# Gated mix of attention and SwiGLU: both parts of a weight made by GpSimd instead of ScalarE and GpSimd

## The chip, the cores and the metric

The kernel runs on one core of a Trainium2 chip. The metric is the device time of one execution in microseconds; several executions are timed and the median is given. One more execution is recorded by the profiler, and all rows shown come from such recordings. The engines of a core are TensorE (PE, with PEld for its weight loads), VectorE (DVE), ScalarE (ACT), GpSimd (POOL) and SyncE (SP), each with an instruction queue of its own that is worked off in order.

## What is computed

The input x has 2048 rows of 640 numbers. One branch is causal attention with 32 heads of 20 numbers in four segments of 512 rows, each with a memory of the segments before it; the other is a SwiGLU feed-forward layer of width 1728. A gate per row mixes the two. All data is f32.

```python
x = A_x
g = _sigmoid((x * gate_w).sum(-1, keepdims=True))
a = _A_ref(x, A_wq, A_wk, A_wv, A_wo, A_beta)   # per segment: softmax attention and memory read, mixed; then @ wo
b = _B_ref(x, B_w1, B_w3, B_w2)                 # (silu(x @ w1) * (x @ w3)) @ w2
return g * a + (1 - g) * b
```

## The kernel before

**Two parts of every operand.** Projections run on PE in the type fp32r. For precision every f32 operand is split: the high part is the value rounded to fp32r, the low part is the value minus the high part. A product takes three matmuls (high by high, high by low, low by high), so each weight tile of 128 by 640 becomes a tile `W` of two parts. The helper `split` (line 115) makes them: line 116 rounds on ScalarE, line 117 subtracts on GpSimd (on VectorE for the first seven weights). The same helper splits `ht`, the product of the feed-forward layer.

**The weights' way.** There are 133 weight tiles in a fixed list of use. `w_load` (line 163) starts the DMA of a raw tile `wr` into one of two raw buffers; `w_split` (line 177) makes `W` from it in one of six slots; `w_step` (line 184) is called at every step of the projections and starts both ahead of use. A slot is free when PE has read the weight six places earlier, a raw buffer when the subtraction on GpSimd has read it. For weights from number 7 on, `w_step` also notes one of ScalarE's latest instructions (`last["exp"]`, an exponential of attention, or `last["act"]`), and `behind` (line 105) pins the cast behind it in ScalarE's queue.

**The stages.** The head projects q, v and k of the first two segments (columns "q", "v", "k"). Then attention runs over 32 groups of four heads, and the projections of both branches are woven between its steps: `g` and `u` (line 262) for the feed-forward layer's two inner products, `f` (line 543) for its outer one, `op` (line 793) for attention's. For each group PE makes scores `s` (line 590), whose row maxima VectorE takes (line 597, tile `junk`), and transposed scores `t` (line 623), whose exponentials ScalarE writes to `P` (line 629) and GpSimd masks (line 633); then `o` (line 643) multiplies `P` and v. The memory read is `nd` (line 340), and `normalize` (lines 717 to 725) scales `o`, with a transpose `gt` and a broadcast `rr` in PSUM. The heads' queries and keys `qk` are loaded by DMAs from GpSimd's queue (line 567), the row maxima `mr` by DMAs from ScalarE's (line 611). After attention a tail ends the last group.

**Order.** PE's order is the program's own. For the other engines a planner at build time sets the order in which their instructions stand in their queues, from its own estimate of when each can run. The eight PSUM banks are handed out in turn (`bank_tile`), so a matmul into a bank waits until the engine that reads its last content is done.

Of the kernel before, what the change touches and what calls it, by code (L numbers as in the profile page):

```python
# [8 lines left out]
F32 = mybir.dt.float32  # L9
# [19 lines left out]
NP, AGE = 3, 4  # L29
# [9 lines left out]
def gated_mix(ctx: ExitStack, tc: tile.TileContext, xT, wqk, wv, w13, w2, w2h, wo, beta, out):  # L39
    nc = tc.nc  # L40
# [61 lines left out]
    here = tc.keep_in_program_order  # L102
    last = {}

    def behind(ins):

        def pin(i):
            if ins is not None:
                tc.add_manual_dep(i.ins, ins.ins.name,
                                  mybir.DependencyInfo(mybir.DependencyClass.NoSync, mybir.DependencyReason.DATA),  # L110
                                  reason="behind")
            return i
        return pin

    def split(dst, src, lo=None, pin=lambda ins: ins):
        pin(nc.scalar.copy(dst[:, 0], src))  # L116
        (lo or nc.gpsimd.tensor_sub)(dst[:, 1], src, dst[:, 0].bitcast(F32))  # L117
# [44 lines left out]
    early, raws, clock = [], [], dict(step=0, oldest=0, next=0)  # L162

    def w_load():
        k = clock["next"]
        src, n, queue = items[k]
        if k in EARLY:
            if k % 2 == 0:
                early[:] = [sp.tile([P, 2, 1280], F32, tag="P32", name=f"wr{k}", bufs=NP)]
            raw = early[0][:, k % 2]  # L170
        else:
            raw = sp.tile([P, D + 2], F32, tag="wraw", name=f"wr{k}", bufs=NRAW)
        queue.dma_start(raw[:, :n], src)
        raws.append([k, raw, n, clock["step"], None])
        clock["next"] += 1

    def w_split():
        k, raw, n, _, after = raws.pop(0)
        w = sp.tile([P, 2, D + 2], FR, tag="W", name=f"W{k}", bufs=NW)
        tiles[k] = w  # L180
        split(w[:, :, :n], raw[:, :n], lo=nc.vector.tensor_sub if k < 7 else None, pin=behind(after))

    def w_step():


        clock["step"] += 1
        for r in raws:
            if clock["step"] - r[3] == (AGE // 2 if "exp" in last else 2 * AGE) and r[0] >= 7:
                r[4] = last.get("exp", last["act"])
        if raws and raws[0][0] in EARLY:  # L190
            if clock["step"] >= 6 + 2 * raws[0][0]:
                w_split()
        elif raws and raws[0][0] < clock["oldest"] + NW and \
                clock["step"] - raws[0][3] >= (AGE if "exp" in last or raws[0][0] < 7 else 2 * AGE + 1):
            w_split()
        if sum(r[0] not in EARLY for r in raws) < NRAW and clock["next"] < min(len(items), clock["oldest"] + NW + NRAW):
            w_load()

    def w_get(i, oldest=None):

        while i not in tiles:
            if not raws or raws[-1][0] < i and len(raws) < NRAW:
                w_load()
            else:
                w_split()
        clock["oldest"] = i if oldest is None else oldest
        return tiles[i]
# [6 lines left out]
    def load_first(c, n):  # L214

        for kb in range(KB):
            r = xraw[c][:, kb]
            nc.sync.dma_start(r, xT[c, :, kb, :])
            split(Xs[c][:, :, kb, :], r, lo=nc.vector.tensor_sub)
            if kb < n:  # L220
                w_load()
                w_split()
# [231 lines left out]
    def job_read(c):  # L454
        return 5.6, memory_read(c)
# [440 lines left out]
    r = job_read(2)  # L896
    up = [job_up(B, 0), job_up(B, 1)]
    seg += q[:2] + [braid(chain(q[2:]), r, 2, 7, False)]
    r = 0.6 * r[0], r[1]
# [17 lines left out]
    for n, (_, g) in enumerate(head):  # L917
        for _ in g:
            stores()
            w_step()  # L920
        if n == 0:
            constants()
        elif n == 4:
            selection()
        elif n == 9:
            gates()
# [9 lines left out]
    def step(run):  # L936
        d = next(run[1], None)
        if d is not None:
            for k in held:
                held[k] += d  # L940
            if not isinstance(d, float):
                stores()
                w_step()
        return d
# [32 lines left out]
    for _, g in tail:  # L977
        for d in g:
            if not isinstance(d, float):
                w_step()  # L980
                tick()
# [51 lines left out]
```

## Time and profile before

| | us |
|---|---|
| runs timed | 1112.77, 1113.28, 1115.76 |
| median | 1113.28 |
| profiled execution, its own time | 1111.06 |
| its span, first to last instruction | 1109.3 |
| busy: PE / PEld / DVE / ACT / POOL | 1094.8 / 853.0 / 588.4 / 461.3 / 493.8 |
| casts of weights on ScalarE (line 116), 133 | 95.7 |
| subtractions for weights on GpSimd (line 117), 126 | 197.7 |

The busy times are sums over one engine's instructions; engines run side by side. An idle time belongs to the engine in whose row it stands, and what ended it is named behind an arrow. A group's row has the line of the kernel, engine, operation, the tile written and those read (buffer numbers left out), shapes, the count, busy us, the mean ns of one, and the idle us before them with what ended it. A row of the timeline has start and duration in us, then the same, and in brackets the idle time before it.

### The profile page before, as it was taken

To read this page: it belongs to the slowest core of one execution; us is meant where nothing else is said; L and a number is where in the kernel's file an instruction comes from. 1 tells how busy PE (TensorE), PEld (TensorE's weight loads), DVE (VectorE), ACT (ScalarE), POOL (GpSimd) and SP (SyncE) were. 2 spreads that over 40 slices of the span, in tenths; PEclk is the share of its full clock that TensorE was granted. 3 is DMA by queue.
4 is the path that set the end of the run, shared out by engine and by line. 5 is a ranking of instruction groups with operands and counts; after the bars stand their busy time and mean duration, and the time that the engine had idled before them with its cause. 6 is when DMAs were issued, how large, how long until landed. Compare 5 with 4: busy or idle time off the path is not lost.

```text
span 1109.3 us, 17962 instructions
## 1 busy us (share of the span) xinstructions
PE 1094.8 (99%) x6285; PEld 853.0 (77%) x6285; DVE 588.4 (53%) x1708; ACT 461.3 (42%) x952; POOL 493.8 (45%) x603
## 2 busy tenths in 40 slices
PE   9999999999999999999999999999999999999997
PEld 6988877777777777787977777777777777777786
DVE  5032564355555554366153677874557665551645
ACT  6265344444244233265254653435543443344130
POOL 5053445355355253354163436544744455354132
PEclk9999999999999999999999999999999999999999
DMA  8265943335165233436276866454744434332123
GB/s 321 94 235 196 278 119 93 82 84 132 47 157 128 60 84 114 123 101 190 94 250 222 290 206 183 112 160 130 182 120 111 123 82 122 84 113 76 51 60 114
DMA packets 87545, 153.20 MB, mean 138 GB/s; under 512 B 11584, under 2 KB 25184, under 8 KB 87456
## 3 DMA queue, kind: packets, MB, share of 16 engines
q1 hardware_dynamic: 63040, 106.30, 30.3%
q0 software_dynamic: 20384, 38.68, 15.6%
q10 hardware_dynamic: 4032, 7.08, 1.8%
q8 instruction: 50, 0.82, 0.3%
q14 instruction: 39, 0.32, 0.1%
HBM read 96.56 MB, written 54.54 MB: 136 GB/s over the span
## 4 chain that ended last, share of the span: by engine, by line
PE 88%; DVE 4%; issue 2%; DMA 2%; ACT 2%; POOL 1%; ACTq 0%; SPq 0%; DVEq 0%; POOLq 0%
PE g L262 16%; PE f L543 16%; PE u L262 15%; PE v L373 6%; PE k L262 6%; PE q L262 6%; PE o L643 5%; PE op L793 5%; PE s L590 4%; PE t L623 3%; PE nd L340 1%; PE pm L437 1%; DVE junk L597 1%; DMA qk<-mr 1%; PE pkt L422 1%
## 5 line engine op out<-in xcount | busy, mean ns | idle before, releaser
L117 POOL TENSOR_TENSOR W<-wr,W 128x640 fp32r<-128x640 f32 (+1 forms) x126 | 197.7, 1575 | 279.3 <-ACT W L116 217.7
L597 DVE CUSTOM_DVE_ANT_0 junk<-s,mask 128x256 bf16<-128x256 f32 (+3 forms) x512 | 250.2, 489 | 106.7 <-PE s L590 73.4
L629 ACT ACTIVATE P<-t 128x512 f32<-128x512 f32 (+1 forms) x384 | 172.4, 538 | 147.9 <-PE t L623 126.3
L262 PE MATMUL g<-X,W 128*128 128x512 f32 x840 | 208.7, 398 | 1.8 <-ACT P L629 1.8
L262 PE MATMUL u<-X,W 128*128 128x512 f32 x780 | 196.8, 399 | 0.0
L543 PE MATMUL f<-ht,W 128*128 128x512 f32 x820 | 196.3, 396 | 0.0
L262 PEld LDWEIGHTS g<-X,W 128*128 128x128 f32 x840 | 155.9, 188 | 38.6 <-ACT P L629 2.0
L633 POOL TENSOR_SCALAR_AFFINE_SELECT P<-P 128x256 f32<-128x256 f32 x192 | 93.3, 496 | 201.7 <-ACT P L629 201.0
L543 PEld LDWEIGHTS f<-ht,W 128*128 128x128 f32 x820 | 152.7, 188 | 36.4
L262 PEld LDWEIGHTS u<-X,W 128*128 128x128 f32 x780 | 144.0, 188 | 34.5 <-ACT P L629 0.3
L116 ACT CAST W<-wr 128x640 fp32r<-128x640 f32 (+1 forms) x133 | 95.7, 729 | 128.7 <-DVE acc L551 26.2
L117 POOL TENSOR_TENSOR ht<-ft,ht 128x512 fp32r<-128x512 f32 x52 | 67.8, 1304 | 81.1 <-ACT ht L116 81.0
L567 POOL DMA_DIRECT2D qk<-qkd x128 | 82.8, 648 | 2.2 <-PE t L623 1.7
L590 PE MATMUL s<-qk 60*128 60x256 f32 (+3 forms) x512 | 78.0, 346 | 1.2 <-DVE fu L503 1.0
L262 PE MATMUL k<-X,W 128*128 128x512 f32 x300 | 77.1, 403 | 0.7 <-ACT P L629 0.7
L643 PE MATMUL o<-P,vg 128*32 128x512 f32 (+3 forms) x1024 | 75.5, 435 | 0.2
L262 PE MATMUL q<-X,W 128*128 128x512 f32 x300 | 74.1, 401 | 1.0 <-DVE X L117 0.5
L503 DVE SCALAR_TENSOR_TENSOR fu<-ft,g 128x512 f32<-128x512 f32 x52 | 35.6, 686 | 73.6 <-ACT ft L502 73.2
L373 PE MATMUL v<-W,X 128*128 128x320 f32 (+1 forms) x480 | 71.6, 311 | 0.4 <-ACT P L629 0.4
L373 PEld LDWEIGHTS v<-W,X 128*128 128x128 f32 x480 | 71.0, 189 | 0.8 <-ACT P L629 0.6
L551 DVE TENSOR_TENSOR acc<-f,acc 128x512 f32<-128x512 f32 x65 | 44.6, 689 | 44.8 <-PE f L543 44.6
L262 PEld LDWEIGHTS q<-X,W 128*128 128x128 f32 x300 | 55.8, 189 | 16.3 <-DVE X L117 1.1
(117 smaller groups left out, 1122.5 us busy)
## 6 DMA issues: line engine op xcount, KB each, us to landing
qk<-qkd POOLq DMA_DIRECT2D x128, 240.0 KB, 4.2
wr<-in_w_dram SPq DMA_DIRECT2D x80, 320.0 KB
qkd<-qs SPq DMA_DIRECT2D x20, 512.0 KB
qkd<-ks SPq DMA_DIRECT2D x20, 512.0 KB
od<-oq SPq DMA_DIRECT2D x32, 256.0 KB
wr<-in_wo_dram SPq DMA_DIRECT2D x20, 320.0 KB
vg<-vd SPq DMA_DIRECT2D x16, 336.0 KB
xr<-in_xT_dram SPq DMA_DIRECT2D x20, 256.0 KB
```

Source lines behind the costliest of these rows:

```text
L116: pin(nc.scalar.copy(dst[:, 0], src))
L117: (lo or nc.gpsimd.tensor_sub)(dst[:, 1], src, dst[:, 0].bitcast(F32))
L262: nc.tensor.matmul(ps, w[:, a, kb * P:(kb + 1) * P], x[:, b, kb, :], start=n == 0, stop=n == 14)
L373: nc.tensor.matmul(ps[:, :n1 - n0], x[:, a, kb, lb * P:(lb + 1) * P], wvt[kb][:, b, n0:n1], start=n == 0, stop=n == 14)
L543: nc.tensor.matmul(ps, w, h, start=n == 0, stop=n == len(ms) - 1)
L567: here(nc.gpsimd.dma_start(t[64 * i:64 * i + RH], qkd[c][RH * (h + i):RH * (h + i + 1)]))
L590: nc.tensor.matmul(ps[i][:, o:o + w], q[:, qb * P:(qb + 1) * P], key[:, :w], start=n == 0, stop=n == len(todo) - 1, skip_group_check=True)
L597: nc.vector.tensor_tensor_reduce(out=junk[:, :w], in0=ps[i][:, o:o + w], in1=mask[:, L - w:], scale=1.0, scalar=-3.0e38, op0=ALU.add, op1= ...
L629: last["exp"] = nc.scalar.activation(pairs[2 * m + k]["P"][:, i, o:o + n], ps[i][:, b:b + n], AF.Exp, scale=SCALE)
L633: nc.gpsimd.affine_select(d, d, pattern=[[0, 2], [0, n], [1, P]], base=0, channel_multiplier=-1, compare_op=ALU.is_ge, fill=0.0)
L643: nc.tensor.matmul(ps[32 * i:32 * i + 32, kb * P:], heads[2 * p + i]["v"][:, kb], pairs[p + i // 2]["P"][:, i % 2, o:o + n], start=kb == 0 ...
L793: nc.tensor.matmul(ps, ws[kb][:, b, fb * P:(fb + 1) * P], oT[a][:, kb], start=n == 0, stop=n == 14)
```

## The change

For weights from number 7 on, the rounded part is made by a copy on GpSimd, directly followed in the program by the subtraction that GpSimd made before. ScalarE keeps the casts of the first seven weights, of x and of `ht`. The pinning of casts falls away with them. 126 instructions move from ScalarE to GpSimd; the planner then sets the queues' orders anew, while PE's order stays as it is.

```diff
-    def behind(ins):
-
-        def pin(i):
-            if ins is not None:
-                tc.add_manual_dep(i.ins, ins.ins.name,
-                                  mybir.DependencyInfo(mybir.DependencyClass.NoSync, mybir.DependencyReason.DATA),
-                                  reason="behind")
-            return i
-        return pin
-
     def split(dst, src, lo=None, pin=lambda ins: ins):
         pin(nc.scalar.copy(dst[:, 0], src))
         (lo or nc.gpsimd.tensor_sub)(dst[:, 1], src, dst[:, 0].bitcast(F32))
...
     def w_split():
-        k, raw, n, _, after = raws.pop(0)
+        k, raw, n, _ = raws.pop(0)
         w = sp.tile([P, 2, D + 2], FR, tag="W", name=f"W{k}", bufs=NW)
         tiles[k] = w
-        split(w[:, :, :n], raw[:, :n], lo=nc.vector.tensor_sub if k < 7 else None, pin=behind(after))
+        if k < 7:
+            split(w[:, :, :n], raw[:, :n], lo=nc.vector.tensor_sub)
+        else:
+            nc.gpsimd.tensor_copy(w[:, 0, :n], raw[:, :n])
+            nc.gpsimd.tensor_sub(w[:, 1, :n], raw[:, :n], w[:, 0, :n].bitcast(F32))
 
     def w_step():
 
 
         clock["step"] += 1
-        for r in raws:
-            if clock["step"] - r[3] == (AGE // 2 if "exp" in last else 2 * AGE) and r[0] >= 7:
-                r[4] = last.get("exp", last["act"])
```

More of the change, by code (lines that the diff above doesn't have):

```diff
@@ L173, in w_load @@
         queue.dma_start(raw[:, :n], src)
-        raws.append([k, raw, n, clock["step"], None])
+        raws.append([k, raw, n, clock["step"]])
         clock["next"] += 1
     def w_split():
-        k, raw, n, _, after = raws.pop(0)
+        k, raw, n, _ = raws.pop(0)
         w = sp.tile([P, 2, D + 2], FR, tag="W", name=f"W{k}", bufs=NW)
         tiles[k] = w
-        split(w[:, :, :n], raw[:, :n], lo=nc.vector.tensor_sub if k < 7 else None, pin=behind(after))
+        if k < 7:
[3 more added lines that the diff above has]
+            nc.gpsimd.tensor_sub(w[:, 1, :n], raw[:, :n], w[:, 0, :n].bitcast(F32))
     def w_step():
         clock["step"] += 1
-        for r in raws:
-            if clock["step"] - r[3] == (AGE // 2 if "exp" in last else 2 * AGE) and r[0] >= 7:
-                r[4] = last.get("exp", last["act"])
         if raws and raws[0][0] in EARLY:
```

## The prediction

> **What bounds the kernel now.** I read the page's first part, then busy time by stretches, then the list of TensorE's (PE's) waits, and only then the two groups that the change touches.
>
> ```profile
> span 1109.3 us, 17962 instructions
> PE 1094.8 (99%) x6285; PEld 853.0 (77%) x6285; DVE 588.4 (53%) x1708; ACT 461.3 (42%) x952; POOL 493.8 (45%) x603
> ...
> 10.00:1100.00 1090.00, 1083.27 (x6252) 847.10 (x6252) 577.52 (x1692) 455.43 (x944) 485.77 (x585) 1.00 0.48 137
> ...
> PE g L262 <- ACT P L629: 1.8, 1, 1.8
> PE nd L340 <- ACT P L629: 1.1, 1, 1.1
> ...
> PE k L262 <- ACT P L629: 0.7, 1, 0.7
> PE t L623 <- DMA qk<-mr: 0.6, 1, 0.6
> ...
> PE v L373 <- ACT P L629: 0.4, 1, 0.4
> ```
>
> PE is busy for 1094.8 of 1109.3 us; between 10 and 1100 us (the third line; its second number is PE's busy time) it is idle for 1090.00 - 1083.27 = 6.7 us, at a granted clock of 1.00. So no relief of another engine can give more than about 6.7 us, 0.6%, and a loss has no such cap. Each row of waits reads: who waited, for whom, us in total, times, longest. Four of them, 1.8 + 1.1 + 0.7 + 0.4 = 4.0 us, are waits for ScalarE (ACT) to take the attention's exponentials (line 629) out of PSUM. No row of the list names a weight tile W: PE never waits for the thing that the change makes in another way. What the change can give is what ScalarE's casts do to its own queue.
>
> **The change, part by part.** The columns here are: engine, operation, tile and shape, count, busy us, mean ns of one, idle us before them and what ended that.
>
> ```profile
> L117 POOL TENSOR_TENSOR W<-wr,W 128x640 fp32r<-128x640 f32 x121 | 189.4, 1571 | 266.4 <-ACT W L116 209.1 <-issue 49.6 <-PE s L590 6.3
> ...
> L78 POOL CAST qk<-one 128x512 fp32r<-128x512 f32 x4 | 2.3, 602 | 0.0
> ...
> L449 POOL COPY Ms<-mt 128x147 f32<-128x147 f32 x4 | 1.2, 304 | 0.1
> ...
> L116 ACT CAST W<-wr 128x640 fp32r<-128x640 f32 x123 | 88.6, 728 | 127.4 <-DVE acc L551 26.2 <-PE u L262 24.8 <-DMA wr<-in_w_dram 19.2
> ```
>
> ScalarE loses 126 of 133 casts (the first seven weights stay): 126 x 0.73 = 92 us, and with them most of the 127 us in which it stood before a cast whose slot or raw weight was not there. GpSimd (POOL) gains 126 copies. Their price is not shown at this width. The cast of 512 columns takes 602 ns and the copy of 147 takes 304, that is 0.82 ns a column, so 640 columns take 0.71 us. The bounds: 0.60 (the 512 columns' own time) and 1.57 (the subtraction of the same tile, which reads two inputs); I take 0.71, because the cast is the same operation. GpSimd goes from 494 to 494 + 126 x 0.71 = 583 us, 53% of the span: no bound by its share. A weight's two parts take 2.28 us in one queue, where the subtraction used to follow 0.73 us of ScalarE; the 209 us that GpSimd stood waiting for ScalarE cover the difference.
>
> Now the places where PE stands still because of a cast.
>
> ```profile
> 929.43 0.73 ACT L116 CAST W<-wr 128x640 fp32r<-128x640 f32 x1
> ...
> 929.68 0.50 PE L623 MATMUL t<-qk 62*128 62x512 f32 x2
> ...
> 931.59 0.72 ACT L116 CAST W<-wr 128x640 fp32r<-128x640 f32 x1 [1.43 <-DMA wr<-in_w_dram]
> ...
> 932.22 2.18 ACT L629 ACTIVATE P<-t 128x512 f32<-128x512 f32 x6
> ...
> 932.86 1.89 PE L262 MATMUL g<-X,W 128*128 128x512 f32 x7 [1.80 <-ACT P L629]
> ```
>
> The scores t are there at about 930.2. ScalarE works in order, stands until 931.59 for a raw weight that is still on its way, casts it, and reads t only at 932.22; PE gets the bank at 932.86. Without the cast the exponentials start at 930.2, the bank is free before PE asks: 1.80 us gained.
>
> ```profile
> 749.84 0.72 ACT L116 CAST W<-wr 128x640 fp32r<-128x640 f32 x1 [0.41 <-DMA wr<-in_w_dram]
> ...
> 750.48 2.18 ACT L629 ACTIVATE P<-t 128x512 f32<-128x512 f32 x6
> ...
> 751.12 0.99 PE L340 MATMUL nd<-Ms,pq 128*128 128x84 f32 x6 [1.06 <-ACT P L629]
> ...
> 560.81 1.39 ACT L116 CAST W<-wr 128x640 fp32r<-128x640 f32 x2
> ...
> 562.05 2.23 ACT L629 ACTIVATE P<-t 128x512 f32<-128x512 f32 x6
> ...
> 562.75 1.43 PE L262 MATMUL k<-X,W 128*128 128x512 f32 x5 [0.71 <-ACT P L629]
> ```
>
> The same twice: 0.41 + 0.72 us of waiting and casting stand ahead of exponentials that PE then waits 1.06 us for; two casts of 1.39 us stand ahead of a wait of 0.71. Gained: 1.06 and 0.71.
>
> ```profile
> 500.77 0.69 DVE L525 TENSOR_TENSOR acc<-acc,sh 128x512 f32<-128x512 f32 x1 [1.69 <-DMA sh<-ed]
> ...
> 511.16 1.57 PE L623 MATMUL t<-qk 62*128 62x512 f32 x6
> ...
> 515.04 0.73 ACT L116 CAST W<-wr 128x640 fp32r<-128x640 f32 x1 [0.55 <-DMA wr<-in_wqk_dram]
> ...
> 516.91 1.89 PE L373 MATMUL v<-W,X 128*128 128x320 f32 x11 [0.42 <-ACT P L629]
> ...
> 701.53 1.28 DVE L723 TENSOR_TENSOR on<-on,gt 128x512 f32<-128x512 f32 x2
> ...
> 702.29 0.63 PE L623 MATMUL t<-qk 62*128 62x512 f32 x6
> ...
> 702.72 0.68 DVE L509 SCALAR_TENSOR_TENSOR ft<-fu,u 128x512 f32<-128x512 f32 x1
> ...
> 702.95 2.36 PE L643 MATMUL o<-P,vg 128*32 128x512 f32 x32
> 703.32 0.68 DVE L597 CUSTOM_DVE_ANT_0 junk<-s,mask 128x512 bf16<-128x512 f32 x1
> ```
>
> Outside PE the order is planned at build, and the plan moves a few VectorE (DVE) instructions too; two of these moves touch PE. First, at 511.16 six t matmuls take 1.57 us that take 0.63 at 702.29: 0.94 us behind a VectorE that is busy without a break since 500.77, where it stood 1.69 us for a transfer (sh). In the changed order two subtractions for X and an addition stand ahead of the multiplication that waits for sh, which fills that gap. With the 0.42 us at 516.91 that is 1.36; the bounds are 0.2 (only what the cast at 515.04 delays) and 1.36; I take 1.3, as the moved work, two or three times about 0.68 us, covers it. Second, a loss: at 701.53 two additions (line 723) free PE's transpose banks by 702.81, and o starts at 702.95. In the changed order the second stands behind the activation's product (L509) and a row maximum (L597): from 702.81 it ends some 0.68 + 0.68 + 0.08 = 1.4 us later, and o waits for that bank. Some of it falls into short waits that PE has anyway just behind; I take 1.0, between 0 and 1.5.
>
> GpSimd's queue is in order as well: a copy that waits for a slot holds what stands behind it. Masks and ht's low parts move by 1 to 3 us by the durations above, and nobody on PE waits for those. The loads of queries and keys are the item with a date.
>
> ```profile
> 936.87 1.29 POOL L567 DMA_DIRECT2D qk<-qkd  x2
> ...
> 952.31 0.50 PE L590 MATMUL s<-qk 60*128 60x512 f32 x2
> ...
> qk<-qkd POOLq DMA_DIRECT2D x128, 240.0 KB, 4.2
> ```
>
> With 4.2 us from issue to landing, this pair must be issued by 948.1 for the s at 952.31. It is issued at 936.87; in the changed order it stands behind both parts of two weights and most of two more, and comes, by my sum, at 947.5 and 948.1: the 11 us of slack are just used up. It costs 0 to 0.5 us; I take 0.
>
> The sum: 1.80 + 1.06 + 0.71 + 1.3 - 1.0 = 3.9 us. The profiled execution took 1111.06 us, 1.8 more than its span, which becomes 1107.2. The median of the runs shown, 1113.28, is 2.2 above it; on that level the forecast is **1109.4 us**, 0.35% faster.
>
> **A rule that speaks against it.**
>
> ```profile
> 506.77 0.68 DVE L525 TENSOR_TENSOR acc<-acc,sh 128x512 f32<-128x512 f32 x1
> ...
> 507.63 3.58 POOL L117 TENSOR_TENSOR W<-wr,W 128x642 fp32r<-128x642 f32 x2 [6.96 <-ACT W L116]
> ...
> 508.57 1.20 DVE L525 TENSOR_TENSOR acc<-acc,sh 128x512 f32<-128x512 f32 x1
> ```
>
> A VectorE product of two SBUF tiles takes 0.68 us alone and 1.20 under a GpSimd subtraction. The Trainium skill, GPSIMD Engine Reference, sections "Engine selection" and "Key points", gives ordinary elementwise work to VectorE and says that GpSimd shares its SBUF interfaces with it, so that VectorE instructions with two SBUF inputs contend; the rows agree. By that rule each such instruction that meets one of the 126 copies is late by up to 0.5 us, and one in the full stretch at 702 would make it 1109.9. By the rows of the sum it stays at 1109.4: the row maxima, which read PSUM and SBUF, are most of VectorE's time, and no copy is seen beside VectorE in this trace.
>
> **The rivals.** *The relief is given back* (0.31): PE's waits for ScalarE go, but VectorE's stretch at 500 stays, 1.80 + 1.06 + 0.71 + 0.2 = 3.8, and the moved addition at 702 costs its full 1.5 and the late load 0.5: 1.8 us gained, 1111.5. For it: two moves outside the casts decide. Against it: VectorE's gap of 1.69 us is plain.
>
> *GpSimd's queue becomes the gate* (0.17, slower): wherever three weight slots come free together, after each of the eight down projections inside attention, two weights' copies and subtractions can go ahead of a pair load. By the sum above such a load is in time at 0.71 us a copy and late by about the excess beyond it. Eight places with 0.9 us each are 7.2 us against 3.9 gained: 1113.28 + 3.3, and with the moved addition at its full 1.5, 1117. It decides from a copy of about 1.6 us, the 1.57 of the two-input subtraction; the 602 ns row of the same operation speaks against it.
>
> *The change does not do what it says*: the built order shows all 126 copies on GpSimd and none of these casts on ScalarE. I give it nothing.
>
> **How the numbers follow.** A measurement of this kernel can tell 0.3%, 3.3 us, from no change. Forecast and what lies beyond it 0.52, given back 0.31, gate 0.17; so faster 0.52, same 0.31, slower 0.17. Low end: all gains without the loss, and the 0.6 us wait for mr too, 5.5 us, and a spread of 1.3 us as the runs show it: 1106.5. High end: the gate in half of its places, with the runs' spread: 1115. The range holds both the forecast and the first rival.
>
> **What would show it.** Right: ACT about 370 us busy with seven W casts, POOL about 583 with 126 copies of 0.71 us; PE's idle time from 10 to 1100 us near 3 us; no PE wait for P above 0.5 us; the t matmuls near 511 at 0.63; o near 702 late behind line 723. Wrong: copies over 1.5 us, PE waiting for qk or W, or the waits for P still there with another holder of ScalarE.

## The result and the profile after

The changed kernel takes 1109.87 us (median of 7 runs, 1108.01 to 1111.02) where the kernel before, beside it, takes 1114.33 (7 runs, 1112.77 to 1115.76): the ratio is 0.9972, 95% interval 0.9959 to 0.9986. A second measurement gave 1109.13 against 1112.63, ratio 0.9968 (0.9955 to 0.998). The forecast was 1109.4.

The page and the stretch from 10 to 1100 us of the changed kernel (columns as in the prediction; lines stand nine lower than before, so 629 is now 620):

```profile
span 1107.7 us, 17867 instructions
PE 1094.4 (99%) x6285; PEld 852.9 (77%) x6285; DVE 592.6 (53%) x1708; ACT 381.2 (34%) x826; POOL 584.7 (53%) x729
```

```profile
10.00:1100.00 1090.00, 1084.92 (x6260) 848.66 (x6259) 583.32 (x1694) 375.34 (x818) 577.88 (x712) 1.00 0.48 137
```

GpSimd is busy for 584.7 us (583 predicted), ScalarE for 381.2. PE's idle time between 10 and 1100 us went from 6.7 to 5.1 us only, and the profiled execution took 1109.41 us, 1.65 less than the one of before, while the medians differ by 4.5 and 3.5. The groups of GpSimd, then PE's waits:

```profile
L174 POOL CAST W<-wr 128x640 fp32r<-128x640 f32 x121 | 87.4, 726 | 199.0 <-PE f L534 41.4 <-issue 26.8 <-PE op L784 20.0
```

```profile
PE o L634 <- DVE on L714: 1.4, 1, 1.4
PE s L581 <- DVE m L588: 1.0, 1, 1.0
...
PE v L364 <- ACT P L620: 0.3, 1, 0.3
PE f L534 <- POOL W L175: 0.3, 1, 0.3
```

A copy costs 726 ns. PE's waits for ScalarE at g, nd and k are gone; new ones stand in the list: o for VectorE, s (its row is read below), and f for a weight. The place that gave most, near 932, from the timeline:

```profile
928.97 2.19 ACT L620 ACTIVATE P<-t 128x512 f32<-128x512 f32 x6 [0.89 <-PE t L614]
...
929.69 3.73 PE L253 MATMUL g<-X,W 128*128 128x512 f32 x15
```

ScalarE now stands ready when the scores come, and g starts without a wait. PE's order is the same in both profiled executions, so their matmuls can be laid side by side, one by one; where the difference of their starts changes, time is gained or lost. It changes by -0.53 us near 512, -0.68 at k (562.75), -0.87 at 680, -1.14 at nd (751) and -1.87 at g (932); and against them by +1.35 at o (702), of which 0.19 comes back just behind, +1.47 at s (952), +0.61 at f (450) and +0.33 near 892.

### The profile page after: what moved, and what is told of

Same layout as the page of the kernel before. It is cut to its first block, busy times and chain, and to the rows that moved or that the text cites. A ratio compares the mean times of both kernels' runs of the same rounds, so it can differ in the third digit from the quotient of the medians.

```text
span 1107.7 us, 17867 instructions
## 1 busy us (share of the span) xinstructions
PE 1094.4 (99%) x6285; PEld 852.9 (77%) x6285; DVE 592.6 (53%) x1708; ACT 381.2 (34%) x826; POOL 584.7 (53%) x729
## 4 chain that ended last, share of the span: by engine, by line
PE 91%; DVE 4%; DMA 1%; ACT 1%; issue 1%; POOL 1%; SPq 0%; ACTq 0%; DVEq 0%; POOLq 0%
PE f L534 16%; PE g L253 16%; PE u L253 15%; PE v L364 6%; PE k L253 6%; PE op L784 6%; PE o L634 6%; PE q L253 6%; PE s L581 5%; PE t L614 4%; PE nd L331 1%; PE pm L428 1%; DVE junk L588 1%; PE pkt L413 1%; PE gt L713 1%
## 5 line engine op out<-in xcount | busy, mean ns | idle before, releaser
L175 POOL TENSOR_TENSOR W<-wr,W 128x640 fp32r<-128x640 f32 (+1 forms) x126 | 200.3, 1596 | 2.3
L174 POOL CAST W<-wr 128x640 fp32r<-128x640 f32 (+1 forms) x126 | 91.0, 726 | 207.5 <-PE f L534 46.9
L493 ACT ACTIVATE ft<-g 128x512 f32<-128x512 f32 x52 | 31.2, 599 | 125.7 <-PE g L253 114.7
L106 ACT CAST ht<-ft 128x512 fp32r<-128x512 f32 x52 | 32.2, 619 | 111.9 <-DVE ft L500 111.8
```

The costliest lines, as they stand in the source:

```text
L174: nc.gpsimd.tensor_copy(w[:, 0, :n], raw[:, :n])
L175: nc.gpsimd.tensor_sub(w[:, 1, :n], raw[:, :n], w[:, 0, :n].bitcast(F32))
```

## The experiments

Theory A: the gain comes from the order in ScalarE's queue (a cast that waits for its raw weight stands ahead of exponentials), and the losses from the order on VectorE and GpSimd. Rival B: ScalarE's lighter load. Rival C: GpSimd is near to being the gate. Rival D: the dropped pins alone.

### Eight casts instead of 126

```diff
+FEW = (67, 70, 71, 83, 91, 92, 112, 113)
-        split(w[:, :, :n], raw[:, :n], lo=nc.vector.tensor_sub if k < 7 else None, pin=behind(after))
+        if k in FEW:
+            nc.gpsimd.tensor_copy(w[:, 0, :n], raw[:, :n])
+            nc.gpsimd.tensor_sub(w[:, 1, :n], raw[:, :n], w[:, 0, :n].bitcast(F32))
+        else:
+            split(w[:, :, :n], raw[:, :n], lo=nc.vector.tensor_sub if k < 7 else None, pin=behind(after))
```

> The kernel before, with only eight of the 126 weights made wholly by GpSimd: those whose ScalarE cast stood ahead of a late attention operation in the trace of before (the weights cast at 515.0, 560.8, 561.4, 669.0, 747.7, 749.8, 929.4 and 931.6 us). Theory A, the order: the gain comes from ScalarE no longer standing in its queue ahead of exponentials that PE waits for; then these eight give nearly all of it, 0.47 at 511 + 0.7 at 562 + 0.8 at 680 + 1.1 to 1.3 at 751 + 1.8 at 932 = 4.9 us, and without the late pair load and the late addition of the changed kernel. So it is as fast as the changed kernel or up to 1 us faster: 1109.0 to 1110.5 us, ratio to before 0.9955 to 0.997. Rival B, the load: the gain comes from ScalarE's 92 us less work; eight casts are 5.8 us, 6 per cent of it, so 0.3 us: ratio 0.9997, no difference.

Measured: 1107.03 us, ratio 0.9952 (0.994 to 0.9965). Repeated beside another row of kernels:

> The kernel of the eight weights once more, as the measure for the others of this row: 1106.5 to 1108.5 us, ratio to before 0.994 to 0.9965.

Measured: 1106.78 us, ratio 0.9955 (0.994 to 0.997). The first one's page and PE's whole list of waits:

```profile
span 1104.9 us, 17961 instructions
PE 1094.5 (99%) x6285; PEld 852.9 (77%) x6285; DVE 590.5 (53%) x1708; ACT 456.0 (41%) x944; POOL 499.3 (45%) x611
```

```profile
PE warm L874 <- DVE zero L871: 1.3, 1, 1.3
PE s L595 <- DVE fu L508: 1.0, 1, 1.0
PE v L378 <- ACT P L634: 0.4, 1, 0.4
PE q L267 <- DVE X L118: 0.4, 2, 0.2
PE q L267 <- ACT X L117: 0.3, 1, 0.3
PE t L628 <- DVE pk L301: 0.3, 1, 0.3
PE t L628 <- DVE pq L301: 0.2, 1, 0.2
```

ScalarE keeps 456.0 of its 461.3 us, and the span falls by 4.4. Side by side with before, PE's difference has four steps and no other above 0.2 us: -0.67 at k (562), -0.88 at 680, -1.14 at nd (751), -1.87 at g (932). Those are the four places named in advance; the fifth, at 511, gave nothing. Six per cent of the relief give more than all of it: rival B falls, and theory A holds with its sizes. (The repeat's profiled execution took 1109.85 us; the last section reads its trace.)

### The load without the wait

```diff
+    idle = cp.tile([P, P], BF, name="idle")
             nc.gpsimd.tensor_sub(w[:, 1, :n], raw[:, :n], w[:, 0, :n].bitcast(F32))
+            for _ in range(3):
+                here(nc.scalar.copy(idle, ident))
```

> The changed kernel, and for each of the 126 weights ScalarE also makes three copies of a constant 128x128 tile into a tile that nobody reads (some 0.26 us each by the copies of 128 to 147 columns, 0.8 us a weight, a little more than the cast's 0.73), at the place of the old cast in program order but with nothing to wait for. ScalarE's busy time is back at 475 to 485 us. Theory A, the order and its waits: a copy that waits for nothing delays an exponential by at most 0.8 us, and those have slack nearly everywhere, so 1110 to 1111.5 us, most of the gain stays; PE's waits for ScalarE's P are at most 0.8 us each. Rival B, the load: the gain is gone, 1113.5 to 1115 us, ratio to before 0.9995 to 1.001.

Measured: 1111.69 us, ratio 0.9986 (0.9973 to 0.9999), between the two theories. The trace tells more. PE's longest waits and the group of copies:

```profile
L178 ACT CAST idle<-ident 128x128 bf16<-128x128 f32 x378 | 113.1, 299 | 27.5 <-DMA qk<-mr 11.9 <-issue 5.1 <-DMA out_dram<-acc 2.7
```

```profile
PE q L256 <- ACT X L107: 1.4, 1, 1.4
...
PE f L537 <- DVE X L133: 1.2, 1, 1.2
...
PE v L367 <- ACT P L623: 0.5, 1, 0.5
```

ScalarE is as loaded as before (478.7 us busy), and PE waits for its P once, 0.5 us. This execution is 2.2 us longer than the changed kernel's, and all of it arises at the first projections, before the first of the added copies. Behind them gains and losses cancel: 1.4 us are lost near 505, where f waits for a part of X, as the planner put VectorE's work there in another order, and 0.3 each near 518, where v waits for P, and 680, where the load of the row maxima is issued later; 0.6 each are gained at 450 and 512 and 0.9 at o. At k, nd and g, where most of the gain was made, the load costs nothing that the trace shows. The median alone would not have decided it; it is likely drawn up by the start (last section): of the twelve runs the three with a mean granted clock of at least 0.999 take 1108.54 to 1109.74 us, the six with at most 0.997 take 1111.70 to 1116.13.

### The pins alone

```diff
-        split(w[:, :, :n], raw[:, :n], lo=nc.vector.tensor_sub if k < 7 else None, pin=behind(after))
+        split(w[:, :, :n], raw[:, :n], lo=nc.vector.tensor_sub if k < 7 else None)
```

> The kernel before without the pins: all casts stay on ScalarE, but nothing holds a cast behind the last exponentials. The built order differs from before in one cast ahead of the attention. Theory A: no difference, ratio 0.999 to 1.001. Rival D, that the pins alone cost the time and dropping them was the gain: ratio 0.996.

Measured: 1112.71 us, ratio 1.0004 (0.9992 to 1.0016). No difference; rival D falls.

### The two late places

```diff
-            here(nc.gpsimd.dma_start(t[64 * i:64 * i + RH], qkd[c][RH * (h + i):RH * (h + i + 1)]))
+            ld = nc.gpsimd.dma_start(t[64 * i:64 * i + RH], qkd[c][RH * (h + i):RH * (h + i + 1)])
+            if "sel" in last:
+                behind(ld, last["sel"])
+            else:
+                here(ld)
...
-                nc.vector.tensor_add(o, o, pt)
+                last["add"] = nc.vector.tensor_add(o, o, pt)
...
+                if "add" in last:
+                    behind(red, last["add"])
```

Here `last["sel"]` is the latest mask of P, `red` a row maximum (the activation's product has the same two lines), and `behind` sets the order in the queue alone.

> The changed kernel with its two late places mended by order alone: a load of queries and keys is held behind the last mask of the scores ahead of it on GpSimd instead of behind every weight part recorded before it, and row maxima and the activation's product stay behind the addition that frees the transpose bank. By the traces the changed kernel lost 1.25 us at o near 702 and 1.28 us at s near 952. Theory A, these two are the losses and each is a matter of order: 2.0 to 2.5 us faster than the changed kernel, PE's waits of 1.4 (o) and 1.0 (s) gone, 1107.0 to 1108.0 us where the changed kernel stands at 1109.9, ratio to before about 0.994 to 0.996. Rival, the losses come from GpSimd's greater load itself: no difference from the changed kernel.

The measure beside it:

> The changed kernel once more, as the measure for the others of this row: 1108.5 to 1110.5 us, ratio to before 0.996 to 0.9985.

Measured: 1107.83 us, ratio 0.9956 (0.9944 to 0.9968), against 1109.13 and 0.9968 (0.9955 to 0.998) for the changed kernel. 1.3 us of the 2.0 to 2.5 show in the medians, and the intervals overlap. In the traces both steps are there: side by side with the changed kernel PE gains 1.0 at 702 (0.8 with what follows just behind) and 1.47 at 950; the wait of o falls from 1.4 to 0.4 us, that of s is gone. The 0.6 at f (450) come back too: PE's wait for a weight there is gone, one of the two loads that GpSimd issued ahead of that weight's subtraction being out of its way. This profiled execution lost 3.7 us at its start (below, under the hardware). So each loss is a matter of order; the sum on the clock is shown less sharply than the steps.

### The transfer before 511

```diff
     def load_raw(c):
...
         xraw[c] = rs
+        if c == 3:
+            load_share(0)
...
-            if c in last:
+            if c in last and c not in shares:
                 load_share(c)
```

The second part keeps the transfer from being made twice.

> The kernel of the eight weights, with one transfer issued earlier: the gate's share that VectorE multiplies by near 500 (sh) is asked for some thirty ScalarE instructions before, with the raw input of the next chunk. The prediction held that VectorE's stand before sh is what makes the t matmuls and v near 511 late by 0.94 + 0.42 us. Theory A: VectorE no longer waits for sh (0.91 us there with the eight weights), so it is that much ahead at 511: the attention block there, 1.57 us over its least, comes to 0.6 or less, 0.9 us faster than the eight-weight kernel, 1106.0 to 1107.0. Rival: VectorE is late there because of its own work and the order of it, and the wait only moves; the block keeps 1.0 to 1.6 us, no difference.

Measured: 1106.06 us, ratio 0.9949 (0.9933 to 0.9966), beside 1106.78 for the eight-weight kernel: 0.7 us less, within the spread. Side by side PE gains 1.08 us near 512, of which 0.14 goes again just behind, and loses 0.36 at another place, near 807; VectorE's timeline has no wait for sh left:

```profile
498.86 1.01 DVE L532 TENSOR_TENSOR acc<-acc,sh 128x512 f32<-128x512 f32 x1
499.80 0.68 DVE L531 TENSOR_TENSOR acc<-f,acc 128x512 f32<-128x512 f32 x1
```

The attention block at 511 (from s to v) takes 5.14 us where it took 6.07 with the eight weights; the like block near 680 takes 4.50, so 1.57 us above that have become 0.64. Theory A holds there in the trace; its median is the lowest of all kernels that ran, but the step is too small for the medians to show.

### How far GpSimd is from being the gate

Three kernels make the copy longer by writing all of it, or the first columns, a second time:

```diff
             nc.gpsimd.tensor_copy(w[:, 0, :n], raw[:, :n])
+            nc.gpsimd.tensor_copy(w[:, 0, :n], raw[:, :n])
```

The other two have `:320` and `:64` in the added line.

> The changed kernel with each GpSimd copy of a weight made twice (the same result written again), so a weight's first part costs GpSimd 1.44 instead of 0.72 us; GpSimd's busy time goes from 585 to about 676 us, 61 per cent. Theory A, GpSimd has room and only loads of queries and keys that stand behind weights are late: the load at 944 comes another 0.7 to 1.5 us later and its s with it, and some of the other seven places with three free slots lose the like: 1111 to 1114 us. Rival C, GpSimd's queue is near to being the gate, as the prediction's rival puts it, deciding from about 1.6 us a copy: eight places with up to 0.9 us each, 1115 to 1118 us, slower than before.

> The changed kernel, and GpSimd makes the first 320 of the 640 columns of each copy again (the same result written again): 0.72 + about 0.42 = 1.14 us a weight, GpSimd busy for about 636 us. The question is where the late loads begin to decide. If time goes with the added work, 53 us more give half of the 95 us: 1150 to 1165 us. If there is a point up to which the slack of 11 us covers it, as the prediction had it at 1.6 us, then few of the ten places are late: 1112 to 1125 us.

> The changed kernel, and GpSimd makes the first 64 of the 640 columns of each copy again: by the copies of 128x147 (0.30 us) some 0.2 us a weight, 25 us in all, GpSimd busy for about 608 us. Half a copy more cost 60 us and a whole one 96, about one us for each us added. If the changed kernel already stands at that slope, 1133 to 1138 us. If it has a margin and the slope begins behind it, 1110 to 1116 us. The order on PE, VectorE and ScalarE is the changed kernel's but for two early copies.

Measured, with the two copies' mean durations from the groups of each kernel:

| columns again | us a weight for both copies | median us | ratio (95%) |
|---|---|---|---|
| 640 | 0.72 + 0.74 | 1205.24 | 1.0826 (1.0808 to 1.0843) |
| 320 | 0.72 + 0.47 | 1169.51 | 1.0509 (1.0496 to 1.0523) |
| 64 | 0.73 + 0.25 | 1123.93 | 1.0109 (1.0085 to 1.0132) |
| none | 0.73 | 1109.13 | 0.9968 (0.9955 to 0.998) |

The whole second copy costs 96 us, where theory A expected at most 5 and rival C 9. Half the columns cost 60, in proportion to the added time (0.47 against 0.74 us) and above both expectations, and 64 columns 14.8, between the two. In the execution with the whole copy PE stands still 65 us longer than in the changed kernel's, and its 6285 matmuls take 31 us longer, at a mean granted clock of 0.964 (last section). Yet GpSimd is busy for only 664.5 of 1203.7 us in the longest of them. PE's waits of that kernel:

```profile
PE s L582 <- DMA qk<-qkd: 38.4, 11, 13.0
PE op L785 <- POOL W L176: 8.5, 4, 4.1
PE f L535 <- POOL W L176: 6.8, 3, 2.6
PE v L365 <- POOL W L176: 5.4, 2, 3.9
```

Besides 38.4 us for loads of qk, PE waits 24.0 us for weights in all (one more such row has 3.3). The loss lies at about eleven places of 2.5 to 19 us each, and with 64 columns 8.4 of 13.0 us lie at one. GpSimd's timeline of that kernel, then PE's:

```profile
947.00 0.71 POOL L174 CAST W<-wr 128x640 fp32r<-128x640 f32 x1
949.12 0.72 POOL L174 CAST W<-wr 128x640 fp32r<-128x640 f32 x1 [1.41 <-DMA wr<-in_w_dram]
...
952.30 0.41 POOL L175 CAST W<-wr 128x64 fp32r<-128x64 f32 x2
952.66 1.56 POOL L176 TENSOR_TENSOR W<-wr,W 128x640 fp32r<-128x640 f32 x1
954.16 1.31 POOL L559 DMA_DIRECT2D qk<-qkd  x2
...
959.12 0.76 PE L582 MATMUL s<-qk 60*128 60x512 f32 x1 [5.32 <-DMA qk<-qkd]
961.49 0.76 PE L582 MATMUL s<-qk 60*128 60x512 f32 x1 [1.61 <-DMA qk<-qkd]
```

The plan puts the casts of two weights ahead of the load. The second stands for its raw weight, whose transfer is issued at 945.84, as soon as the subtraction that ends at 945.81 has given a raw buffer back; the load stands behind all of it. The same pair was issued at 943.79 in the changed kernel. The planner set GpSimd's order anew in each of these kernels: here ht's subtraction stands behind both casts, in the changed kernel between them. So the table gives the price of a longer copy together with the order that the planner then makes; a longer copy in an unchanged order was not run. Is it only the loads' place in the queue? The load is held behind the mask, as above, in the kernels with 64 and with 640 columns again:

> The kernel with 64 columns of each copy made again (1124 us), and the loads of queries and keys held behind the last mask of the scores instead of behind all weight parts recorded before them. By its trace 9 of the 13 us that it lost stand at s near 959, which waits 5.3 us for a load that stands behind the parts of two weights. Theory A, at this load GpSimd still makes the weights in time and only the loads behind them are late: 1108 to 1113 us. Rival C, the weights themselves are late by now, as with the doubled copies, where freeing the loads gave back only 16 of 96 us: 1118 us or more.

> The kernel with each GpSimd copy made twice (1205 us), and the loads of queries and keys held behind the last mask of the scores instead of behind all weight parts recorded before them. Theory A, order: the 92 us of the doubled copies are loads of queries and keys stuck behind weight parts, which in turn stand for their raw weight; freed from that, PE's 38 us of waits for qk and most of what follows from them go: 1110 to 1140 us, what is left being waits for W. Rival C, throughput: GpSimd cannot make two weights in the time that the plan leaves, whatever the order of the loads: 1180 us or more, PE's waits for W in the place of those for qk.

Measured: 1110.32 us, ratio 0.9986 (0.9975 to 0.9998), with 64 columns: 13.6 of the 14.8 us come back, as theory A has it, and so does a wait of 1.3 us for a weight at v. But 1189.0 us, ratio 1.0683 (1.067 to 1.0697), with 640: freeing them gave back 16 of 96, and there theory A fell. PE's waits for weights stay where they were, 24.4 us in all, for instance at the output projection, which needs five of them one behind the other. PE's list, then its timeline:

```profile
PE s L592 <- DMA qk<-qkd: 15.5, 4, 13.4
PE rr L719 <- DMA rR<-rp: 11.4, 2, 6.8
```

```profile
441.21 0.50 PE L795 MATMUL op<-oT,W 128*128 128x512 f32 x1 [1.96 <-POOL W L182]
...
445.53 0.80 PE L795 MATMUL op<-oT,W 128*128 128x512 f32 x1 [3.59 <-POOL W L181]
```

Two things keep the rest from coming back. 14.9 of the 15.5 us for qk are the first group's loads, which have no mask ahead of them and so stay where they stood: the edit didn't free them. And late weights hold up another queue: the transfers of rR (the broadcast's input) stand in SyncE's queue behind transfers of raw weights, which wait for GpSimd to give a buffer back. In the timeline a subtraction on GpSimd ends at 749.19, the raw transfer behind it is issued at 749.22, rR's at 749.61, some 20 us after their data was written, and PE has waited 6.84 us when rr starts at 753.12.

So both are true in turn. A little above the present price the load's place in the queue makes nearly all of the loss; at twice the price the weights themselves come late in the bursts, whatever the order of the loads. How much of the 96 us the late return of raw buffers makes stays open; a third raw buffer was not tried.

## Why the prediction was right, and where it wasn't

*The gains at ScalarE* were sized well: 1.80, 1.06 and 0.71 us against 1.87, 1.14 and 0.68, and the eight-weight kernel shows that they come from these casts and no others. The wait for mr, which the prediction put into the low end alone, gave 0.87: ScalarE's cast of the row maxima no longer stands behind a weight's.

*The term at 511 was the worst:* 1.3 taken between 0.2 and 1.36, and 0.53 came. The step that failed is that the moved subtractions fill VectorE's gap before sh. They are there, but ScalarE issues the transfer of sh later (497.50 instead of 496.73), its data is there 4.5 us after that instead of 4.0, and VectorE still stands:

```profile
499.90 0.68 DVE L515 TENSOR_TENSOR acc<-f,acc 128x512 f32<-128x512 f32 x1
502.03 1.29 DVE L516 TENSOR_TENSOR acc<-acc,sh 128x512 f32<-128x512 f32 x2 [1.44 <-DMA sh<-ed]
```

That sh was the cause was right: issued earlier, it gave 0.9 us. The edit under study just didn't do that.

*The loss at 702* was 1.35, or 1.16 with what came back just behind, for the 1.0 taken, by the mechanism named.

*The load at 944* was taken at 0 and cost 1.47. Its timeline in the changed kernel:

```profile
943.79 1.31 POOL L558 DMA_DIRECT2D qk<-qkd  x2
...
949.13 0.50 PE L581 MATMUL s<-qk 60*128 60x512 f32 x1
950.63 0.47 PE L581 MATMUL s<-qk 60*128 60x512 f32 x1 [1.00 <-DVE m L588]
```

The pair's second half, issued at 944.44, lands at about 950.5, where PE goes on. The row names VectorE's m, which ended at 950.53, just as near; but that m is the row maximum of the first s, and before, both s start at 952.31 without it. A second trace of the changed kernel names the load, and there it landed in 5.3 us and cost 0.7:

```profile
950.39 0.46 PE L581 MATMUL s<-qk 60*128 60x512 f32 x1 [0.23 <-DMA qk<-qkd]
```

The prediction read another pair as the one that decides. The pair whose landing starts s is the later of two (in the 64-column kernel each s starts 0.13 us after one of its halves lands); in the kernel before it is this one, not that of 936.87:

```profile
940.82 1.27 POOL L567 DMA_DIRECT2D qk<-qkd  x2
```

So the slack was 7.3 us by the prediction's own 4.2, not 11. Three things used it up: the load was issued 3.0 us later, the gains brought PE to s 3.2 us sooner, and the second half took 6.0 us to land instead of 4.3. By 4.2 us, the median, it would still have been in time, at 948.6; what failed is that step.

*A weight that comes late* is a term that the prediction put at nothing, as no wait of PE named a W. In the changed kernel f at 450 waits 0.33 us for the low part of one, and 1.05 in the second trace; the 0.61 us lost there in the first are gone where the loads are held behind the mask. In the second trace:

```profile
450.83 3.52 PE L534 MATMUL f<-ht,W 128*128 128x512 f32 x14 [1.05 <-POOL W L175]
```

*The sum and the level.* The terms promised 3.9 us between the two profiled executions and 1.65 came: 0.8 short at 511, 1.5 at the load, 0.6 at f, 0.3 near 892 and 0.2 at 702; 0.9 over at mr, and 0.1 each at the start and at nd, g and k together. The forecast still met the median, because that stands 2.2 us above the profiled execution for before and only 0.5 for the changed kernel. That part was luck. Of the runs with a mean granted clock of at least 0.999 in the second measurement, five of the changed kernel lie at 1108.02 to 1109.27 and three of before at 1111.46 to 1111.89, some 3 us apart, so the two profiled executions show less of the gain than the runs do; at f and s two executions of the changed kernel alone differ by 0.7 and 0.8 us, in opposite directions.

*The rule on contention*, weighed against the change: VectorE's busy time rose from 588.4 to 592.6 us, and to 597.8 with all copies made twice. That is little for 91 us of copies each time. The product that reads sh kept its mean (866 and 851 ns), a subtraction of two SBUF tiles (`oall` from `on` and `gm`) went from 796 to 871 ns, and to 1003 with the copies made twice; no run separates what of it is the copies'. The row maxima, which the prediction calls most of VectorE's time, are 250 of its 588 us.

*The rivals.* "Given back" described the balance well in kind (order on VectorE and a late load take back a part), at less than its price. The gate didn't close, but the prediction's point for it, a copy of about 1.6 us, was far too high: it begins at 0.73, where a load costs 1.5 us in one execution and 0.7 in another, and costs 15 us at 0.98 and 96 at 1.46, where the prediction had 7 for all. Its mistake was to count only a load's own lateness, and not the raw buffer returned late, the next copy that stands for it, the weights that are late themselves, and PE's clock behind a long wait.

## What to carry to other kernels

Look first for instructions that wait, in an engine's queue, ahead of work that the bound engine needs: moving eight of 126 gave more than moving all. Give the engine that takes work over a margin in its bursts, not in its share: here one at 53% was 0.25 us a weight, and the order that the planner made for it, from losing 15 us. And take the landing of a transfer that has just enough time from the slow end of its group, not from the median.

## What the runs showed of the hardware

A wait of PE can cost more than its length. In the execution with both places mended, PE waited 1.42 us for the first X at 9.41; the stretches of 4 us (the last three numbers are granted clock, DMA share and GB/s; the first after the comma is PE's busy time):

```profile
4.00:8.00 4.00, 3.62 (x10) 1.21 (x7) 2.36 (x3) 1.92 (x3) 0.91 (x2) 1.00 1.00 337
8.00:12.00 4.00, 2.45 (x5) 1.66 (x6) 2.98 (x5) 3.60 (x6) 1.09 (x2) 0.66 1.04 398
12.00:16.00 4.00, 4.00 (x10) 3.09 (x10) 1.71 (x3) 2.04 (x5) 1.49 (x2) 0.50 1.00 373
16.00:20.00 4.00, 4.00 (x18) 3.22 (x17) 2.27 (x4) 2.21 (x5) 3.29 (x3) 0.98 0.64 246
```

The clock falls to 0.50 for about 4 us and more, and PE falls 3.7 us behind the changed kernel's profiled execution, which has a granted clock of 1.00 in each of these stretches and its longest wait there at 0.43 us; about 1 us of it is longer waits, the rest comes behind them, with PE busy. Two more traces show it at the same place. The repeat of the eight-weight kernel waited 0.94 us at 8.95, had clocks of 0.75 and 0.83 in the second and third stretch, and lost 2.1 us there against the first execution of the same kernel; the kernel with ScalarE's added copies waited 1.40 us at 9.02 and lost 2.2 against the changed kernel. Since runs of one kernel with a lower mean clock are mostly the longer ones, this is likely a part of their spread. The clock is not all of it: in the same repeat t at 632.68 waits 0.95 us for the load of the row maxima, where the first execution doesn't wait, and 1.0 us more is lost at a clock of 1.00.

The clock also falls behind the long waits for late loads (near 959 in the 64-column kernel):

```profile
950.00:956.00 6.00, 3.80 (x17) 2.73 (x15) 1.71 (x3) 0.62 (x1) 4.92 (x7) 0.98 0.13 18
956.00:962.00 6.00, 1.27 (x3) 0.82 (x5) 0.70 (x2) 0.00 (x0) 3.51 (x4) 0.50 1.07 249
962.00:968.00 6.00, 6.00 (x51) 3.07 (x48) 1.76 (x4) 2.68 (x6) 0.84 (x2) 0.66 0.09 36
```

It need not be a long one. In that kernel s waits 0.89 us at 127.34 for its load, and in the one with the loads freed 0.90 us at 127.64. The stretch behind it, in the first and in the second:

```profile
128.00:132.00 4.00, 4.00 (x18) 3.27 (x18) 2.76 (x9) 1.61 (x3) 1.47 (x3) 1.00 0.78 300
```

```profile
128.00:132.00 4.00, 4.00 (x14) 3.06 (x11) 2.26 (x8) 0.00 (x0) 0.00 (x0) 0.57 0.81 316
```

The second lost 1.9 us more. And the waits of 1.4 us at o and 1.80 at g cost no more than their length. The Trainium skill, TensorE: Matmul & The Clock Gate, section "HAM oscillation — how this bites in real kernels", puts the rule at idle gaps of about 3.4 us. The traces agree with it for 5.32 us and for 1.80, but not for 0.90, 0.94, 1.40 and 1.42, behind which the clock fell too; the measurement decides, and what made those waits count stays open.
